# A fused attention and state-space kernel: the third state tile's arguments in full-width matmuls, and a new task order

## The chip, the cores and the metric

The kernel runs on one core of one Trainium2 chip. The metric is the time of one execution on the device in microseconds. A core has TensorE (PE, with weight loads shown apart as PEld), VectorE (DVE), ScalarE (ACT), GpSimd (POOL) and SyncE (SP); the last two mainly issue DMAs here.

## The reference

Two branches work on the same x of 2048 rows and 640 channels, and a gate per row mixes them.

```python
def reference(A_x, A_wqkv, A_wo, ..., B_A_re, B_A_im, B_B_re, ..., B_Dskip, gate_w):
    g = _sigmoid((x * gate_w).sum(-1, keepdims=True))
    a = _A_ref(x, A_wqkv, A_wo)     # local attention: 32 heads of 20, 8 positions with stride 2
    b = _B_ref(x, ...)              # state-space convolution
    return g * a + (1 - g) * b

def _B_ref(u, A_re, A_im, B_re, B_im, C_re, C_im, log_dt, Dskip):
    dt = jnp.exp(log_dt)[:, None]
    logdA = dt * A                  # A, B, C complex, 640 channels x 192 states
    P = jnp.exp(logdA[:, :, None] * l[None, None, :])
    K = jnp.einsum("dn,dnl,dn->dl", Cc, P, dB).real
    # y = causal convolution of u with K along 2048 positions, by FFT
    return y + u * Dskip
```

The edit lies in how K is computed: for every channel, a sum over 192 complex states of exponentials at all positions.

## The kernel before

**Stages.** The state's parameters are prepared by elementwise work and written to a DRAM table `Sprm` (12 numbers per state, 192 states per channel). Then a planned stretch, up to about 302 us, mixes four kinds of work on all engines: the projections to q, k and v (L328), the local attention (products L377 and L442, sums L383 and L447, output projection L464), the kernel K of the state branch (class `KGen`, L768 to L826), and the first step of the FFTs (L1195). After it `fft_conv` does the rest of the convolution and the output in the order of the code.

**The order.** In the planned stretch each piece of work is a `Task` with an engine (or a choice of ACT and DVE for evictions from PSUM), a price in us, what it depends on, the buffers it takes and releases, and a due time. `Plan.order` is a list scheduler run while the program is built: it takes the free engine with the earliest start and, among tasks ready there, the one with the least due time. For tasks with a choice of engine `bd` is added to the due time on DVE and `ba` taken off on ACT; `grace` is added for a ScalarE task that needs another activation table. The dictionary `PLAN` holds these numbers, the due times of the stages and offsets of single tasks (`off`). Each engine then executes its tasks in that fixed order, waiting where an input is not there.

**The K stage.** It runs over 10 chunks. A chunk has 8 channels from each of 8 groups (4 groups `g`, each in two halves `v`), 192 states each. `load_L` fetches the chunk's slice of `Sprm` into a tile L with the DMA queue of SP: partitions 0 to 63 hold groups 0 and 2, partitions 64 to 127 groups 1 and 3. There are two L tiles, so the load of chunk c waits for the arguments of chunk c-2.

192 states are one and a half times 128, so the states of a pair of halves are three tiles `u` of 128 partitions. In the tiles 0 and 1 the first 128 states of one half v fill the partitions. Tile 2 has the remaining 64 states of both halves, 64 partitions each. For each tile and chunk there are four sine tasks and two exponent tasks on PE, named arg: a matmul with 64 rows of L as the stationary operand and a constant matrix R (304 or 216 columns) streaming gives the arguments in PSUM, and ScalarE applies Sin (L785) or Exp (L787) to them in one instruction. Tile 0 and 1 use L768, tile 2 uses L773. DVE multiplies the results (L808 to L810) into `pt` and `qq`, and 64 or 128 small matmuls per tile (L826, in four tasks kmm) sum over the states into `kps`, 32 columns of the array per group g. These small matmuls go in tile order 0, 1, 2 and accumulate in the same PSUM bank; for tiles 0 and 1 they contract 128 rows, for tile 2 64 rows.

The attention weights are stored by SP (aS, L419) and read back spread over partitions (asb, L423), on the same queue as L; results of the attention leave by it too (L484). GpSimd's queue carries q, k, v (L343, L368) and the constants of the FFT.

Of the kernel before, what the change touches and what calls it, by code (L numbers as in the profile page):

```python
# [20 lines left out]
S = 2048  # L21
D = 640
# [14 lines left out]
def _attn_consts():  # L37
# [5 lines left out]
    for wp in range(W):  # L43
# [1 line left out]
    return ind.astype(NPBF), ident.astype(NPBF), mask0  # L45


PLAN = dict(free=dict(P=4.0, A=4.2, D=4.7, S=16.0, G=16.0), phase=0.0, look=0.2, ba=85.1, bd=-687.6, grace=2235.8, p0=-791.4, p1=9.6, tx=[1364.4, 1460.7],
            txw=191.1, ql=135.4, vl=-242.7, pw=18.0, el=-653.5, tl=53.4, vw=216.1, gate=2445.0,
            l=[281.2, 189.1, 532.1, 186.3, 592.1, 47.7, -314.8, 735.8, 829.8, 993.2, 720.0, 710.4], a=[363.0, -174.6, -128.2, 185.6, 703.1, 918.9, 1303.1, 1413.4],  # L50
            v=[-164.3, -448.6, 45.4, 323.3, 710.0, 789.4, 646.8, 1095.8], g=[10.7, 292.0, -348.6, -469.5, -539.5, 427.8, 247.2, -1193.3, -158.0, -278.7, -66.5],
            dl=[129.5, 80.5, 337.8, 725.2, 614.9, 306.3, 515.6, 330.1, 400.6, 420.8],
            kl=[-352.8, -363.0, -133.2, -213.8, -584.9, -123.6, 147.3, -7.2, -17.6, -95.2], Ll=1248.1, argl=366.8, xl=1038.4, c0=1194.1, x0=1143.6, x1=118.9,
            f0=-483.5, f1=51.4, u0=914.8, u1=33.6, off={59: 46.6, 61: 84.7, 94: -58.1, 96: -12.9, 100: -8.6, 102: -29.5, 107: 10.3, 111: 11.8, 113: 8.0, 116: -14.8,
            120: 4.2, 124: -16.2, 129: -52.6, 138: -3.1, 140: -39.7, 146: -5.9, 149: -47.1, 157: -75.2, 160: -33.8, 166: -52.0, 173: 27.0, 175: 23.3, 180: -8.6,
            182: -11.7, 186: 12.8, 188: 5.8, 197: 20.3, 198: -7.7, 201: 130.7, 204: -86.5, 206: -14.4, 208: -15.3, 210: -5.1, 212: 12.5, 215: -21.4, 219: 9.3,
            221: 20.7, 223: -12.2, 433: -31.6, 795: 94.5, 1037: 67.6, 1081: -4.5, 1100: 133.0, 1168: -45.3, 1170: 12.6, 1174: 37.0})


class Task:  # L60
# [434 lines left out]
NST = 192  # L495
# [7 lines left out]
NPC = 12  # L503
# [205 lines left out]
class KGen:  # L709
# [24 lines left out]
    def load_L(self, c):  # L734
        nc = self.nc
        L = self.Lb[c % 2]
        for g in range(4):
            for v in range(2):
                d0 = 160 * g + 80 * v + 8 * c
                src = self.prm.S[d0:d0 + 8].rearrange("(s q) i n -> (q i) s n", q=4)  # L740
                nc.sync.dma_start(L[64 * (g % 2) + 2:64 * (g % 2) + 2 + 4 * NPC, g // 2, :, NST * v:NST * v + NST], src)

    def plan(self, pl, pa, pk, start, hold, params, opened, fin):
        nc, R = self.nc, self.R
# [4 lines left out]
        for c in range(NCH):  # L749
            d0, dd = start(c), start(c + 1) - start(c)  # L750
            L = self.Lb[c % 2]
            Lt = pl.add(f"L{c}", "S", 3.5, lambda _, c=c: self.load_L(c), deps=argt[c - 2] if c > 1 else params, due=d0 - pr["Ll"], dma=1.3)
            argt.append([])
            ends, held, k = {}, {}, 0
            b = {"started": set()}
            for kind in (0, 1) if c % 2 == 0 else (1, 0):
                for u in range(3):
                    ends[u, kind] = []
                    for gp in range(2):
                        for sub in range(2) if kind == 0 else (None,):  # L760
                            def args(_, u=u, kind=kind, gp=gp, sub=sub, b=b, L=L):
                                ar = b["ar"] = pa.tile([128, 2, 512], F32, name="ar")
                                for sb, a0 in ((sub, 0),) if kind == 0 else ((0, 0), (1, EW)):
                                    c0, ncol = ((0, SW), (SW, EW))[kind]
                                    for g2 in range(2):
                                        rows = slice(64 * g2, 64 * g2 + 64)
                                        if u < 2:
                                            nc.tensor.matmul(ar[:, g2, a0:a0 + ncol], L[rows, gp, sb, NST * u:NST * u + 128], R[rows, c0:c0 + ncol],  # L768
                                                             start=True, stop=True, tile_position=(64 * g2, 0))
                                        else:  # L770
                                            m0 = NST * gp + 128
                                            for h in range(2):
                                                nc.tensor.matmul(ar[64 * h:64 * h + 64, g2, a0:a0 + ncol], L[rows, h, sb, m0:m0 + 64], R[rows, c0:c0 + ncol],  # L773
                                                                 start=True, stop=True, tile_position=(64 * g2, 64 * h))
                                b["ar", u, kind, gp, sub] = ar

                            def act(_, u=u, kind=kind, gp=gp, sub=sub, b=b):
                                opened()
                                ar = b.pop(("ar", u, kind, gp, sub))
                                if gp == 0 and not sub:  # L780
                                    b["T", u, kind] = self.ring[kind][self.turn[kind] % len(self.ring[kind])]
                                    self.turn[kind] += 1
                                dst = b["T", u, kind]
                                if kind == 0:
                                    nc.scalar.activation(dst[:, 2 * gp:2 * gp + 2, sub, :], ar[:].bitcast(I16)[:, :, 0:2 * SW:2], ACT.Sin, scale=SCL)  # L785
                                else:
                                    nc.scalar.activation(dst[:, 2 * gp:2 * gp + 2].rearrange("p g s n -> p g (s n)"), ar[:, :, 0:2 * EW], ACT.Exp)  # L787
                            due = d0 + dd * k / 18.0
                            first = not ends[u, kind]
                            a = pl.add(f"arg{c}{kind}{u}{gp}{sub}", "P", ((0.15, 0.15, 0.30), (0.22, 0.22, 0.40))[kind][u], args, deps=[Lt], after=[prevarg] + ([self.moved] if c == HC + 2 else []), acq=["ar"],  # L790
                                       due=due - pr["argl"], eq=(304, 432)[kind])
                            t = pl.add(f"act{c}{kind}{u}{gp}{sub}", "A", (0.62, 0.83)[kind], act, deps=[a], after=[prevact] + (hold if first and kind == 0 and ns == NTR - 1 else []), acq=[("trg", "exq")[kind]] if first else [],
                                       rel=[("ar", a)], due=due, table=("sin", "exp")[kind])
                            if first:
                                held[u, kind] = t
                                ns += kind == 0
                            prevarg, prevact = a, t
                            argt[c].append(a)
                            ends[u, kind].append(t)
                            k += kind + 1  # L800
            for u in range(3):
# [12 lines left out]
                def kmm(_, u=u, b=b, j=0):  # L814
                    if u == 0 and j == 0:
                        b["kps"] = pk.tile([128, 2, 256], F32, name="kps", tag="kb")
                    pt, qq = b["pq", u]
                    kps, started = b["kps"], b["started"]
                    for ql in (2 * j, 2 * j + 1):
                        for v in range(2):  # L820
                            for c2 in ((u,) if u < 2 else (0, 1)):
                                for g in range(4):
                                    r0 = 0 if u < 2 else 64 * (g // 2)
                                    rows = slice(0, 128) if u < 2 else slice(r0, r0 + 64)
                                    k = 8 * (g if u < 2 else 2 * c2 + g % 2) + ql
                                    nc.tensor.matmul(kps[32 * g:32 * g + 32, c2, NM * ql:NM * ql + NM],  # L826
                                                     pt[rows, k, v, :], qq[rows, k, v, :],
                                                     start=(g not in started), stop=(u == 2 and v == 1), skip_group_check=True,
                                                     tile_position=(r0, 32 * g))
                                    started.add(g)  # L830
                due = d0 + dd * (0.55 + 0.16 * u) + pr["dl"][c]
                p = pl.add(f"pq{c}{u}", "D", 2.04, products, deps=ends[u, 0] + ends[u, 1], after=self.pqs[-1:], acq=["pq"], rel=[("trg", held[u, 0]), ("exq", held[u, 1])], due=due)
                self.pqs.append(p)
                for j in range(4):
                    m = pl.add(f"kmm{c}{u}{j}", "P", 0.18 if u < 2 else 0.35, lambda e, kmm=kmm, j=j: kmm(e, j=j), deps=[p], after=[prevkmm], acq=["kb"] if u == 0 and j == 0 else [],
                               rel=[("pq", p)] if j == 3 else [], due=due + pr["kl"][c] + 0.2 * j, eq=211)
                    if u == 0 and j == 0:
                        m0 = m
# [435 lines left out]
```

## Time and profile before

| what | value |
|---|---|
| median of 3 runs | 385.3 us (383.39 to 386.51) |
| the profiled execution | 384.76 us |
| its span, first to last instruction | 383.0 us |
| mean granted TensorE clock | 0.95 |
| PE busy | 316.9 us |
| DVE busy | 323.0 us |
| ACT busy | 304.1 us |

The span is what the profile covers; the execution's own time is 1.76 us longer. Lines such as L768 are lines of the kernel file. Busy time of a group of instructions is the time in which at least one of them ran. A matmul's own duration in the profile (some 300 ns) is much longer than the distance between two starts, since they overlap; the distance in the timeline is what one costs. The word issue as a releaser stands for time in which the engine waited for nothing that the profile shows.

### The profile page before, as it was taken

What the parts mean: (1) busy time and instruction counts of PE and PEld (TensorE: products, weight loads), DVE (VectorE), ACT (ScalarE), POOL (GpSimd) and SP (SyncE); (2) the same over time, 40 slices, a digit from 0 to 9 for tenths busy, and PEclk for the clock granted to TensorE, in tenths of its full rate; (3) what the DMA queues carried; (4) which work ended last, traced back from release to release, by engine and by line L of the source; (5) the groups of instructions that cost most, each with busy time, mean ns of one, the idle gap of its engine ahead of it and who ended that gap; (6) DMA issues with size and microseconds to landing.
All of it is one profiled execution on the core that took longest, in us unless ns stands there. A gap on an engine that the chain in (4) does not pass through costs nothing.

```text
span 383.0 us, 11863 instructions
## 1 busy us (share of the span) xinstructions
PE 316.9 (83%) x5102; PEld 191.0 (50%) x5126; DVE 323.0 (84%) x437; ACT 304.1 (79%) x427; POOL 89.3 (23%) x122
## 2 busy tenths in 40 slices
PE   0268999998999979988997699889999899987760
PEld 0144564433445545444454344557777655656760
DVE  4879997669999989889998799999896389999782
ACT  1699884677979889789879698988987798995890
POOL 8930331140211001513653100100010022000053
PEclk9998999999999999999989757999999999998996
DMA  8982878472645233686455850403740199926056
GB/s 266 373 252 94 246 212 256 117 215 86 193 125 157 64 112 95 158 224 188 104 124 134 274 154 2 151 2 101 254 140 34 36 211 244 207 40 222 2 119 159
DMA packets 51529, 58.84 MB, mean 154 GB/s; under 512 B 36244, under 2 KB 43284, under 8 KB 51220
## 3 DMA queue, kind: packets, MB, share of 16 engines
q1 hardware_dynamic: 41492, 28.78, 28.3%
q0 software_dynamic: 8256, 28.69, 25.6%
q8 instruction: 40, 0.66, 0.7%
q10 hardware_dynamic: 1728, 0.61, 0.7%
q14 instruction: 13, 0.11, 0.1%
HBM read 38.29 MB, written 19.77 MB: 152 GB/s over the span
## 4 chain that ended last, share of the span: by engine, by line
PE 51%; ACT 19%; DVE 13%; DMA 9%; issue 5%; SPq 1%; POOL 1%; POOLq 0%; ACTq 0%; DVEq 0%
PE tb L328 13%; PE tb L447 7%; PE ar L768 6%; PE fp L1024 5%; PE tb L464 5%; PE kps L826 4%; PE bp L1195 3%; DMA aim<-in_B_A_im_dram 3%; ACT big L787 3%; ACT sp_u L1027 3%; ACT big L785 3%; PE lg L383 3%; DVE bufA L985 3%; ACT sp_k L1027 3%; PE ar L773 2%
## 5 line engine op out<-in xcount | busy, mean ns | idle before, releaser
L328 PE MATMUL tb<-bufA 128*128 128x512 bf16 x283 | 71.5, 388 | 6.5 <-DVE bufA L492 2.1
L785 ACT ACTIVATE big<-ar 128x608 bf16<-128x608 int16 x96 | 59.6, 677 | 10.2 <-PE ar L768 9.4
L787 ACT ACTIVATE big<-ar 128x864 bf16<-128x864 f32 x60 | 50.2, 897 | 4.1 <-PE ar L768 3.3
L442 DVE TENSOR_TENSOR pv<-vc,asb 128x2048 bf16<-128x2048 bf16 x40 | 47.2, 1219 | 4.3 <-PE tb L447 2.1
L328 PEld LDWEIGHTS <-bufA 128*128 128x128 bf16 x300 | 33.2, 120 | 35.1 <-issue 12.2
L377 DVE TENSOR_TENSOR prod<-qc,kc 128x2048 bf16<-128x2048 bf16 x40 | 47.9, 1219 | 2.7 <-PE lg L383 2.5
L768 PE MATMUL ar<-Rarg,L 64*128 64x304 bf16 (+1 forms) x320 | 37.0, 290 | 5.8 <-ACT big L785 2.4
L447 PE MATMUL tb<-pv,ident 128*128 128x512 bf16 (+1 forms) x185 | 39.1, 348 | 2.5 <-DVE prj L492 1.0
L826 PE MATMUL kps<-qq,pt 128*32 128x22 bf16 (+1 forms) x2560 | 30.2, 175 | 4.6 <-issue 4.2
L1024 PEld LDWEIGHTS <-PHI 128*128 128x128 bf16 x256 | 24.8, 97 | 17.6 <-issue 7.4
L826 PEld LDWEIGHTS <-pt 128*32 128x32 bf16 (+1 forms) x2560 | 23.3, 93 | 17.5 <-issue 12.3
L464 PE MATMUL tb<-wo_sb,oT 128*128 128x320 bf16 x160 | 27.7, 310 | 0.0
L768 PEld LDWEIGHTS <-L 64*128 64x128 bf16 x320 | 13.7, 94 | 27.7 <-issue 25.3
L447 PEld LDWEIGHTS <-ident 128*128 128x128 bf16 x192 | 17.8, 99 | 17.3 <-issue 5.5
L490 ACT ACTIVATE prj<-tb 128x512 bf16<-128x512 f32 x28 | 16.5, 598 | 10.9 <-PE tb L328 9.9
L959 POOL DMA_DIRECT2D PHI<-c_phi x8 | 4.5, 558 | 79.5 <-PE fp L1024 41.7
L773 PE MATMUL ar<-Rarg,L 64*64 64x304 bf16 (+1 forms) x320 | 19.6, 298 | 3.8 <-ACT big L787 1.6
L1027 ACT ACTIVATE sp_k<-fp 128x1280 bf16<-128x1280 f32 x16 | 19.1, 1236 | 3.3 <-PE fp L1024 3.0
L810 DVE TENSOR_TENSOR qq<-big 128x1408 bf16<-128x1408 bf16 x24 | 21.3, 886 | 0.0
L1024 PE MATMUL fp<-bufA,PHI 128*128 128x320 bf16 x128 | 19.1, 298 | 2.3 <-ACT sp_u L1027 1.5
L243 PE MATMUL ar<-ident,xn 128*128 128x128 bf16 x80 | 7.9, 263 | 15.6 <-DMA xn<-in_A_x_dram 14.1
L1024 PE MATMUL fp<-big,PHI 128*128 128x320 bf16 x128 | 19.2, 298 | 1.8 <-ACT sp_k L1027 1.8
(201 smaller groups left out, 633.0 us busy)
## 6 DMA issues: line engine op xcount, KB each, us to landing
asb<-aS SPq DMA_DIRECT2D x8, 512.0 KB, 4.0
PSI<-c_psi SPq DMA_DIRECT2D x8, 512.0 KB, 10.2
PHI<-c_phi POOLq DMA_DIRECT2D x8, 384.0 KB, 6.6
Sprm<-pc SPq DMA_DIRECT2D x12, 240.0 KB, 3.7
L<-Sprm SPq DMA_DIRECT2D x80, 36.0 KB, 2.6
kc<-kS POOLq DMA_DIRECT2D x8, 337.5 KB, 4.7
vc<-vS POOLq DMA_DIRECT2D x8, 337.5 KB, 4.9
xn<-in_A_x_dram SPq DMA_DIRECT2D x4, 640.0 KB, 12.4
```

Source lines behind the costliest of these rows:

```text
L328: nc.tensor.matmul(ppf, self.wq[:, kt, which * D + e:(which + 1) * D:5], self.xT[:, c0 // 1024, kt, c0 % 1024:c0 % 1024 + SC], start=(kt = ...
L377: nc.vector.tensor_tensor(b[e][:], b["qc"][:, e, :].unsqueeze(1).to_broadcast([128, W, C]), win(b["kc"][:, e, :], 0, W, DIL, C), ALU.mult)
L442: nc.vector.tensor_tensor(b["pv", e][:, :, k, :].rearrange("p w (b t) -> p w b t", t=64), for_e, aw, ALU.mult)
L447: nc.tensor.matmul(b["op", e][:, 0:n, :], ident[:], b["pv", e][:, w, 0:n, :], start=(w == 0), stop=(w == W - 1))
L464: nc.tensor.matmul(apf[:, :320], b["oT"][:, e, i * 128:(i + 1) * 128], wo_sb[:, e, hf * 320:(hf + 1) * 320], start=(e == 0), stop=(e == 4))
L768: nc.tensor.matmul(ar[:, g2, a0:a0 + ncol], L[rows, gp, sb, NST * u:NST * u + 128], R[rows, c0:c0 + ncol], start=True, stop=True, tile_pos ...
L773: nc.tensor.matmul(ar[64 * h:64 * h + 64, g2, a0:a0 + ncol], L[rows, h, sb, m0:m0 + 64], R[rows, c0:c0 + ncol], start=True, stop=True, til ...
L785: nc.scalar.activation(dst[:, 2 * gp:2 * gp + 2, sub, :], ar[:].bitcast(I16)[:, :, 0:2 * SW:2], ACT.Sin, scale=SCL)
L787: nc.scalar.activation(dst[:, 2 * gp:2 * gp + 2].rearrange("p g s n -> p g (s n)"), ar[:, :, 0:2 * EW], ACT.Exp)
L826: nc.tensor.matmul(kps[32 * g:32 * g + 32, c2, NM * ql:NM * ql + NM], pt[rows, k, v, :], qq[rows, k, v, :], start=(g not in started), stop ...
L1024: nc.tensor.matmul(fp[:, fl, 0:320].rearrange("p (c x) -> p c x", x=32), PHI[:, fl, kind, :], B[:, :, 2 * f1 + ri].rearrange("p c q g -> p ...
L1027: nc.scalar.activation(t[:], fp[:, :, 0:320].rearrange("p f (x g) -> p x f g", g=4), ACT.Identity)
```

## The change

The table L is stored in another order. The 384 columns of L for one half v now hold, in this order: the first two groups' states 0 to 127, then their states 128 to 191 beside the last two groups' states 128 to 191, then the last two groups' states 0 to 127. The groups 2 and 3 therefore come in two DMAs each instead of one. Every tile is now 128 adjacent columns of L, and each argument task has the same two (sine) or four (exponent) matmuls with 128 stationary columns; the branch with four 64x64 matmuls is gone. The mixed tile moves from place 2 to place 1. The tiles now hold other groups: tile 0 the groups 0 and 1 with both v, tile 2 the groups 2 and 3, so their small matmuls go to two of the four column strips; tile 1 has all four groups with 64 rows each. Prices in the plan follow, and all numbers of `PLAN` and its offsets are others.

```diff
-PLAN = dict(free=dict(P=4.0, A=4.2, D=4.7, S=16.0, G=16.0), phase=0.0, look=0.2, ba=85.1, bd=-687.6, grace=2235.8, p0=-791.4, p1=9.6, tx=[1364.4, 1460.7],
...
+PLAN = dict(free=dict(P=4.0, A=4.2, D=4.7, S=16.0, G=16.0), phase=0.0, look=0.2, ba=194.5, bd=1544.6, grace=243.1, p0=-727.2, p1=21.0, tx=[-447.7, -203.8],
...
@@ load_L
                 src = self.prm.S[d0:d0 + 8].rearrange("(s q) i n -> (q i) s n", q=4)
-                nc.sync.dma_start(L[64 * (g % 2) + 2:64 * (g % 2) + 2 + 4 * NPC, g // 2, :, NST * v:NST * v + NST], src)
+                dst = L[64 * (g % 2) + 2:64 * (g % 2) + 2 + 4 * NPC, :, v]
+                if g < 2:
+                    nc.sync.dma_start(dst[:, :, 0:NST], src)
+                else:
+                    nc.sync.dma_start(dst[:, :, NST:256], src[:, :, 128:NST])
+                    nc.sync.dma_start(dst[:, :, 256:2 * NST], src[:, :, 0:128])
@@ plan
-            Lt = pl.add(f"L{c}", "S", 3.5, lambda _, c=c: self.load_L(c), ..., dma=1.3)
+            Lt = pl.add(f"L{c}", "S", 5.4, lambda _, c=c: self.load_L(c), ..., dma=1.5)
...
-                                        if u < 2:
-                                            nc.tensor.matmul(ar[:, g2, a0:a0 + ncol], L[rows, gp, sb, NST * u:NST * u + 128], R[rows, c0:c0 + ncol],
-                                                             start=True, stop=True, tile_position=(64 * g2, 0))
-                                        else:
-                                            m0 = NST * gp + 128
-                                            for h in range(2):
-                                                nc.tensor.matmul(ar[64 * h:64 * h + 64, g2, a0:a0 + ncol], L[rows, h, sb, m0:m0 + 64], R[rows, c0:c0 + ncol],
-                                                                 start=True, stop=True, tile_position=(64 * g2, 64 * h))
+                                        nc.tensor.matmul(ar[:, g2, a0:a0 + ncol], L[rows, sb, gp, 128 * u:128 * u + 128], R[rows, c0:c0 + ncol],
+                                                         start=True, stop=True, tile_position=(64 * g2, 0))
...
-                            a = pl.add(f"arg{c}{kind}{u}{gp}{sub}", "P", ((0.15, 0.15, 0.30), (0.22, 0.22, 0.40))[kind][u], args, ...
+                            a = pl.add(f"arg{c}{kind}{u}{gp}{sub}", "P", (0.15, 0.22)[kind], args, ...
...
-                            for c2 in ((u,) if u < 2 else (0, 1)):
-                                for g in range(4):
-                                    r0 = 0 if u < 2 else 64 * (g // 2)
-                                    rows = slice(0, 128) if u < 2 else slice(r0, r0 + 64)
-                                    k = 8 * (g if u < 2 else 2 * c2 + g % 2) + ql
+                            for c2 in range(2):
+                                for g in range(4) if u == 1 else (u, u + 1):
+                                    r0 = 64 * (g // 2) if u == 1 else 0
+                                    rows = slice(r0, r0 + 64) if u == 1 else slice(0, 128)
+                                    k = 8 * (2 * c2 + g % 2) + ql
                                     nc.tensor.matmul(kps[32 * g:32 * g + 32, c2, NM * ql:NM * ql + NM],
                                                      pt[rows, k, v, :], qq[rows, k, v, :],
-                                                     start=(g not in started), stop=(u == 2 and v == 1), skip_group_check=True,
+                                                     start=(g not in started), stop=(v == 1 and u == 1 + g // 2), skip_group_check=True,
                                                      tile_position=(r0, 32 * g))
...
-                    m = pl.add(f"kmm{c}{u}{j}", "P", 0.18 if u < 2 else 0.35, ...
+                    m = pl.add(f"kmm{c}{u}{j}", "P", 0.35 if u == 1 else 0.18, ...
```

## The prediction

> **What bounds the kernel now.** I read the page's head first, then busy time by stretch, then TensorE's groups with shapes kept apart, then the timeline where its clock is full and where it is halved, and last the DMA queue of SyncE. The head, and the groups of the whole span:
>
> ```profile
> span 383.0 us, 11863 instructions
> PE 316.9 (83%) x5102; PEld 191.0 (50%) x5126; DVE 323.0 (84%) x437; ACT 304.1 (79%) x427; POOL 89.3 (23%) x122
> PE 51%; ACT 19%; DVE 13%; DMA 9%; issue 5%; SPq 1%; POOL 1%; POOLq 0%; ACTq 0%; DVEq 0%
> ```
>
> Three engines are near the same load, and the chain that ended last runs half its time through PE. The planned part holds the change; in the busy times by stretch it splits at 258.3 us, where ScalarE ends its last state activation (columns: stretch, length, busy of PE, PEld, DVE, ACT, POOL, clock, DMA share, GB/s):
>
> ```profile
> 75.00:258.30 183.30, 164.10 (x3607) 85.34 (x3620) 166.63 (x234) 156.74 (x232) 40.28 (x48) 0.93 0.48 134
> 258.30:302.00 43.70, 41.84 (x435) 31.99 (x437) 36.70 (x48) 36.14 (x46) 2.66 (x4) 1.00 0.37 116
> ```
>
> No engine alone sets the first stretch: DVE 91%, PE 90%, ACT 86% of it. The second is PE's, 96% of it. From 302 us on the code is the same. So a saving on PE is worth its full length only where it lets work come forward out of the second stretch.
>
> **The argument matmuls** (L768 tiles 0 and 1, L773 tile 2), in TensorE's groups by shape:
>
> ```profile
> L768 PE MATMUL ar<-Rarg,L 64*128 64x304 bf16 x160 | 23.8, 319 | 4.2 <-ACT big L785 2.4 <-ACT bufA L785 1.2
> L773 PE MATMUL ar<-Rarg,L 64*64 64x304 bf16 x160 | 12.5, 334 | 1.6 <-ACT big L785 1.1
> L768 PE MATMUL ar<-Rarg,L 64*128 64x216 bf16 x160 | 13.2, 261 | 1.6 <-ACT big L787 1.0 <-DVE nxt L492 0.4
> L773 PE MATMUL ar<-Rarg,L 64*64 64x216 bf16 x160 | 7.1, 262 | 2.3 <-ACT big L787 1.6 <-issue 0.5
> L826 PE MATMUL kps<-qq,pt 128*32 128x22 bf16 x1280 | 15.6, 177 | 0.2 <-DVE qq L810 0.2
> L259 PE MATMUL ar<-gw_sb,bufA 128*128 128x1 bf16 x80 | 2.1, 163 | 0.0
> ```
>
> A sine task of tile 0 or 1 is 2 matmuls, so 80 tasks took 23.8 us, 0.298 each; one of tile 2 is 4 matmuls, 40 tasks took 12.5 us, 0.313 each. Exponent tasks: 40 in 13.2 us (0.330) against 20 in 7.1 us (0.355). The four quarter-size matmuls already run beside each other; the third tile is not twice as dear, though the plan has it at 0.30 and 0.40 against 0.15 and 0.22. Making tile tasks alike saves 40 x 0.015 + 20 x 0.025 = 1.1 us of PE in the whole kernel. If every task gained as much as one whole short matmul start of the nearest row (L259, 2.1 us / 80 = 26 ns), the 160 removed matmuls would be worth 4.2 us; that is the far bound. On the other side the saving is nothing, where ACT is what PE waits for (4.2 + 1.6 + 1.6 + 2.3 us of idle stand before these groups, mostly ACT's). I take -0.8, near the direct rows. The 160 weight loads that go with them overlap matmuls and cost nothing; the cover is PEld at 85.3 of 183.3 us, and without it they would be a gain (8.9 us for 320, so 4.5 us).
>
> The Trainium skill ("TensorE: Matmul & The Clock Gate", Wait — 56ns, not 53.3ns?) says starts never come closer than about 25 ns, however short the matmul. By that the sum of this step would be -4.0 instead of -0.8; the trace agrees on the whole array (26 ns above) and disagrees for tiles, as the next lines show.
>
> **The matmuls that form K** (L826). Before, tiles 0 and 1 send each step to all four 32-column strips; after, tiles 0 and 2 use strips 0, 1 or 2, 3, each twice in turn, and tile 1 has the four strips with 64 rows. The counts are the same: 16, 32 and 16 per piece. Timeline, at full clock (190 us) and at half clock (216 us):
>
> ```profile
> 190.02 0.37 PE L826 MATMUL kps<-qq,pt 64*32 64x22 bf16 x32
> 190.36 0.31 PE L768 MATMUL ar<-Rarg,L 64*128 64x304 bf16 x2
> 190.59 0.61 PE L383 MATMUL lg<-prod,ind 128*32 128x512 bf16 x8
> ...
> 191.37 0.37 PE L826 MATMUL kps<-qq,pt 128*32 128x22 bf16 x32
> 191.68 0.30 PE L768 MATMUL ar<-Rarg,L 64*128 64x304 bf16 x2
> 215.88 0.41 PE L826 MATMUL kps<-qq,pt 64*32 64x22 bf16 x33 [2.61 <-issue]
> ...
> 216.59 0.40 PE L826 MATMUL kps<-qq,pt 64*32 64x22 bf16 x32
> 216.92 0.43 PE L768 MATMUL ar<-Rarg,L 64*128 64x304 bf16 x2
> ```
>
> Start to next start: 0.34 us / 32 = 10.6 ns and 0.31 / 32 = 9.7 at full clock, 0.33 / 32 = 10.3 at half clock. A pace that does not move when the clock halves is not set by streaming 22 columns, so four strips are more than it needs, and I cost two strips at nothing. Lower bound: nothing, as no work goes. Upper bound: each matmul waits for its predecessor as on the whole array, 26 ns: 10 chunks x 2 tiles x 64 = 1280 matmuls, each 15.7 ns longer, 20 us of PE. Between these the rows nearest in kind are the 10 ns ones.
>
> **The loads of the table L** (L741). Before 8 DMAs per chunk; after, the upper two groups are cut in two, 12 per chunk. All 40 new ones are issued on SP's queue, POOL's is untouched. From the source view of that line (its instruction, who waited for it in us and times, and landing):
>
> ```profile
> L741 SPq DMA_DIRECT2D L<-Sprm x80: 302/423/1613, 62.6 to 226.7; - x80
> PEld L768: 0.6, 2
> DMA to landing us min/median/max: 1.7/2.6/5.1
> ```
>
> At the median of 423 ns, 4 more are 1.7 us per chunk and 17 us of SP in all. PE waited for a load of L twice, 0.6 us. L for chunk 7 is issued from 184.8 to 189.6 us and first used at 205.1, so 1.7 us hides behind 15 us of the chunk before. What stands behind it on SP is the pair of transfers that spread the attention weights (aS, then asb); at 207.65 an aS store follows an L burst at once. If all 8 blocks stood behind one and DVE had nothing else, 8 x 1.7 = 13.6 us; nothing where they don't. DVE's wait for asb is 1.8 us today, so I take 0. The pieces shrink from rows of 384 bytes to 256 and 128 for half the groups, 36 KB per DMA becoming 24 and 12, hidden by the same lead.
>
> **The order anew.** No task is added or removed; their fixed order is recomputed from new prices and priorities. Evictions that either engine may do lose rank on DVE (bd from -687.6 to 1544.6) and gain it on ACT (ba 85.1 to 194.5), a change of activation table costs less rank (grace 2235.8 to 243.1). DVE was busy 203.3 and ACT 192.9 of the 227 us from 75 to 302, so evening them out is worth up to 5.2 us. 10 ACT table loads stand at the state's two activation lines, at 1.283 us; twice as many would cost ACT 12.8 us, against 34 us idle. PE idles 21.1 us in those 227. The profile cannot say which order is better; its bounds are the cases below, and I take 0.
>
> **Sum.** -0.8 (arguments) + 0 (K) + 0 (loads) + 0 (order) on the profiled execution's own 384.76 us (span 383.0 and 1.76 around it) gives 384.0. The median of the three runs, 385.3, is 0.5 above that execution. Runs differ by 383.39 to 386.51, so about 1% is what a measurement tells from no change.
>
> **Rivals.** *The order fits better*: the 2.61 us in which PE and then every engine waited for issue at 213 us, and the halved clock after it, are not met again, and DVE sheds evictions: 384.0 - 2.6 - 5.2 = 376.2, say 377. For it: 24 us of DVE idle in 227; the clock was halved from 215 to 232 us, where sine tasks took 0.43 us instead of 0.30. Against: DVE was full through that stretch, so the half clock cost little, and the stall ends in issue, which an order does not address.
>
> *The order is built on PE time that does not exist* (slower): the plan's price of the arguments falls by 40 x 0.15 + 20 x 0.18 = 9.6 us, PE's work by 1.1. The other 8.5 us is filled with tasks that come late. In-order queues pass that on: behind a late argument matmul stand ACT's next activation, then DVE's products. Place: the arguments from 75 to 258 us, where ACT already waits 9.4 us for L768. It decides once PE's idle time at those places (9.7 us before the four argument groups) is used up. All of it on the path: 384.0 + 8.5 = 392.5. Against: 21 us of PE idle could take it.
>
> *Two strips are too few* for L826: the 20 us above, of which PE's half of the chain would show, 384.0 + 10 = 394. Against it: the pace at half clock. If 26 ns held for one strip only, two in turn would give 13 ns, 1280 x 2.7 ns = 3.5 us, 386 to 387. By the same section of the skill's page a floor kept by each strip gives this last figure.
>
> *It does not do what it says*: the third tile's tasks are already as short as the others; this is in the forecast, not a separate case.
>
> **How the numbers follow.** Forecast, no measurable change: 0.34, own range 381 to 388. Better order 0.31. Late arguments 0.22. Strips 0.13. The better order may go beyond 377 and the two slower ones may add; I leave 1 in 10 out on each side: 375 to 396. Faster by over 1%: 0.31 + 0.01 of the forecast = 0.32. Slower by over 1%: 0.21 + 0.12 + 0.02 = 0.35. Within: 0.33.
>
> **What would show it.** L768 should have 480 matmuls: 240 of 304 columns near 35.7 us busy and 240 of 216 columns near 19.8; L773's line gone. L826 stays near 10 ns from start to start; 13 or more says strips. 120 issues at L741, with PE's wait for L under 2 us. If ACT's wait for argument matmuls grows well past its 15.9 us (9.4 + 3.3 + 2.3 for L768, 0.7 + 0.2 for L773), the late-argument rival is right. If DVE's idle in the planned part shrinks by 5 us or ACT does more of the evictions, the better order. The forecast is wrong if the planned part, now ending at 302 us, moves by over 4 us.

## The result, and the profile after

The changed kernel takes 401.6 us (median of 4 runs, 400.35 to 405.11) against 385.1 us for the kernel before (4 runs, 383.39 to 386.51). The ratio is 1.0445, 95% interval 1.0363 to 1.0527: slower, where the forecast was 384.0 and the range ended at 396. The profiled execution took 400.35 us, its span is 398.3, 15.3 longer than before. Medians count every run; the ratios leave out runs over 1.5% above the fastest of their kernel.

The head of the page after, with its row of the granted clock in 40 slices (here some 10 us each) and the shares of the chain that ended last:

```profile
span 398.3 us, 11631 instructions
PE 335.4 (84%) x4966; PEld 199.2 (50%) x4966; DVE 319.7 (80%) x428; ACT 316.3 (79%) x438; POOL 83.0 (21%) x122
...
PEclk9999999999999998688955558989999999996996
...
PE 61%; ACT 23%; issue 5%; DMA 4%; DVE 3%; POOL 1%; SPq 1%; POOLq 0%; ACTq 0%
```

The clock row before, for comparison:

```profile
PEclk9998999999999999999989757999999999998996
```

The records hold 136 PE matmuls fewer, and PE is busy 18.5 us longer. Its share of the chain went from 51% to 61%. The clock row after shows a run of fives around 200 to 240 us that the kernel before does not have (its mean clock was 0.950, this one's is 0.906).

The planned part now ends at about 316.8 us instead of 302.0 (its last L1195 matmul at 315.7 instead of 300.6), so nearly all of the 15.3 us lie in it. Its busy times by stretch (stretch, length, busy of PE, PEld, DVE, ACT, POOL, clock, DMA share, GB/s), and the second stretch in the kernel before:

```profile
75.00:316.80 241.80, 219.91 (x3882) 122.25 (x3881) 199.67 (x272) 201.00 (x285) 34.54 (x49) 0.87 0.43 119
200.00:241.00 41.00, 34.12 (x936) 18.35 (x928) 32.89 (x54) 34.27 (x49) 2.35 (x4) 0.50 0.39 110
```

```profile
200.00:241.00 41.00, 33.83 (x815) 16.77 (x814) 35.98 (x52) 34.07 (x50) 6.63 (x12) 0.73 0.49 140
```

PE's idle time in the planned part is 241.8 - 219.9 = 21.9 us; before it was 227.0 - 205.9 = 21.1. So PE does not wait more: it is busy 14.0 us longer with fewer matmuls. Where, say its groups by shape, and the K group of 64 rows in the kernel before:

```profile
L773 PE MATMUL ar<-Rarg,L 64*128 64x304 bf16 x240 | 39.7, 342 | 6.1 <-ACT big L785 3.6 <-ACT bufA L785 1.1 <-ACT big L787 0.9
L826 PE MATMUL kps<-qq,pt 128*32 128x22 bf16 x1280 | 24.9, 176 | 5.5 <-issue 5.5
L773 PE MATMUL ar<-Rarg,L 64*128 64x216 bf16 x240 | 22.9, 284 | 3.3 <-ACT big L787 3.2
L826 PE MATMUL kps<-qq,pt 64*32 64x22 bf16 x1280 | 14.7, 174 | 4.6 <-issue 4.6
```

```profile
L826 PE MATMUL kps<-qq,pt 64*32 64x22 bf16 x1280 | 14.6, 173 | 4.3 <-issue 4.2
```

Two things stand out. The K matmuls of 128 rows took 15.6 us before and take 24.9; those of 64 rows, which still rotate over four strips, took 14.6 and now 14.7. And the argument matmuls take 62.6 us where 35.7 + 19.8 were expected. The timeline of PE, first where the clock is full and then at 223 us, shows both the slower pace and a third thing:

```profile
119.97 0.56 PE L826 MATMUL kps<-qq,pt 128*32 128x22 bf16 x32
120.47 0.30 PE L773 MATMUL ar<-Rarg,L 64*128 64x304 bf16 x2
...
223.54 0.31 PE L826 MATMUL kps<-qq,pt 128*32 128x22 bf16 x10
226.06 0.26 PE L826 MATMUL kps<-qq,pt 128*32 128x22 bf16 x6 [2.21 <-issue]
```

32 K matmuls of 128 rows on two strips last 0.56 us from the first start to the last end; in the kernel before 32 of them on four strips took 0.37 (at 191 us). And in the middle of a run of K matmuls PE stops for 2.21 us on nothing that the profile shows.

**What the stalls are.** In every kernel here, all PE stalls of over 0.45 us before an instruction that waits for no semaphore stand at one and the same remainder when PE's recorded instructions are counted in steps of 256 (a few records are missing, so the remainder drifts by up to 8 within a run). The trace's DMA records have a queue that the page calls q8 instruction; it moves packets of 16,384 bytes, and 39 of them over the run fit PE's 4966 + 4966 instructions in blocks of 256 (38.8). So I read these stalls as ends of a block of the instruction stream: the next block isn't there yet. In all runs here two of these packets never start closer together than 3.28 us. A block of K matmuls alone is 128 matmuls with their weight loads, which take 128 x 7 to 13 ns = 0.9 to 1.7 us, so PE can run ahead of its instructions. The Trainium skill ("Runtime: NRT & Kernel Launch", Instruction fetch mechanics) has the same block, 16 KiB or 256 instructions, and calls the cost of crossing its end "mostly hidden"; the trace agrees on the size and not on the cost, 10.1 us of stalls here.

**What the half clock is.** The trace's clock records say 0.5 or 1.0. From 75 to 317 us the spells at 0.5 last multiples of 3.4 us and sum to 23.9 us before and 61.4 after, 41.0 of it in one spell from 200.3 us. Of the 20 spells of 10 us or more in that stretch of all runs here, 15 begin 1 to 4 us after the start of a stall of over 0.45 us (in the changed kernel a stall from 196.6 to 198.5, then the spell from 200.3); the other five don't. The Trainium skill ("TensorE: Matmul & The Clock Gate", Part 1: The HAM clock gate) describes this gate, half or full by how busy PE was in the last 3.4 us; the lengths of the spells agree. What counts as busy is the question of experiment 9.

Three suspects, then: the strips, the block ends, the order that meets the half clock. The table sums up the runs that follow. Stalls are those of at least 0.15 us without a wait; stalls and half clock are summed from 75 to 317 us of each profiled run. The forms of the runs are explained below; o_old and o_new stand for the old and the new order.

| kernel | median us | ratio to before (95%) | K of 128 rows, busy | stalls | half clock |
|---|---|---|---|---|---|
| before | 385.1 | | 15.6 | 6.2 | 23.9 |
| after | 401.6 | 1.0445 (1.0363 to 1.0527) | 24.9 | 10.1 | 61.4 |
| s_new_o_old | 392.8 | 1.0209 (1.0121 to 1.0298) | 23.5 | 9.2 | 37.5 |
| s_old_o_new | 394.6 | 1.0253 (1.0189 to 1.0317) | 17.1 | 10.2 | 58.0 |
| s_fix_o_old | 386.3 | 1.0015 (0.9968 to 1.0062) | 15.9 | 3.7 | 17.1 |
| s_fix_o_new | 399.5 | 1.0374 (1.0283 to 1.0466) | 17.4 | 15.6 | 54.6 |
| s_fix_8_loads | 388.55 | 1.0030 (0.9992 to 1.0068) | 15.9 | 7.2 | 23.9 |
| s_one_strip | 404.5 | 1.0480 (1.0422 to 1.0537) | 30.4 | 9.0 | 44.4 |
| before, moved by 112 | 401.5 | 1.0395 (1.0349 to 1.0441) | 15.9 | 12.3 | 44.4 |
| before, moved by 160 | 390.0 | 1.0109 (1.0017 to 1.0202) | 16.0 | 8.7 | 27.3 |
| before, moved by 224 | 388.9 | none on record | 15.8 | 7.1 | 20.5 |
| after, moved by 16 | 403.0 | 1.0447 (1.0354 to 1.0540) | 24.9 | 9.9 | 61.4 |
| after, moved by 144 | 404.9 | 1.0495 (1.0400 to 1.0591) | 24.4 | 11.4 | 61.4 |

### The profile page after: what moved, and what is told of

Its sections match the earlier page's. It is cut to its first block, busy times and chain, and to the rows that moved or that the text cites. A ratio compares the mean times of both kernels' runs of the same rounds, so it can differ in the third digit from the quotient of the medians.

```text
span 398.3 us, 11631 instructions
## 1 busy us (share of the span) xinstructions
PE 335.4 (84%) x4966; PEld 199.2 (50%) x4966; DVE 319.7 (80%) x428; ACT 316.3 (79%) x438; POOL 83.0 (21%) x122
## 4 chain that ended last, share of the span: by engine, by line
PE 61%; ACT 23%; issue 5%; DMA 4%; DVE 3%; POOL 1%; SPq 1%; POOLq 0%; ACTq 0%
PE tb L329 12%; PE ar L773 10%; PE tb L448 9%; PE kps L826 8%; PE tb L465 5%; PE fp L1024 5%; PE bp L1195 4%; DMA aim<-in_B_A_im_dram 3%; PE lg L384 3%; ACT big L785 3%; ACT sp_u L1027 3%; ACT big L787 3%; ACT sp_k L1027 3%; ACT big L491 2%; PE cp L1057 2%
## 5 line engine op out<-in xcount | busy, mean ns | idle before, releaser
L329 PE MATMUL tb<-bufA 128*128 128x512 bf16 x300 | 72.4, 386 | 1.1 <-DVE bufA L493 0.5
L785 ACT ACTIVATE big<-ar 128x608 bf16<-128x608 int16 x96 | 61.1, 678 | 13.6 <-PE ar L773 12.0
L773 PE MATMUL ar<-Rarg,L 64*128 64x304 bf16 (+1 forms) x480 | 62.2, 313 | 9.4 <-ACT big L787 4.1
L826 PE MATMUL kps<-qq,pt 128*32 128x22 bf16 (+1 forms) x2560 | 39.3, 175 | 10.1 <-issue 10.1
L826 PEld LDWEIGHTS <-pt 128*32 128x32 bf16 (+1 forms) x2560 | 31.3, 95 | 25.7 <-issue 21.6
L448 PE MATMUL tb<-pv,ident 128*128 128x512 bf16 (+1 forms) x192 | 42.3, 368 | 0.0
L773 PEld LDWEIGHTS <-L 64*128 64x128 bf16 x480 | 20.7, 97 | 42.7 <-issue 38.6
L465 PE MATMUL tb<-wo_sb,oT 128*128 128x320 bf16 x160 | 28.7, 317 | 0.1
L491 ACT ACTIVATE prj<-tb 128x512 bf16<-128x512 f32 x33 | 19.4, 597 | 11.1 <-PE tb L329 9.6
L448 PEld LDWEIGHTS <-ident 128*128 128x128 bf16 x192 | 18.5, 103 | 17.3 <-issue 5.9
L808 DVE TENSOR_TENSOR pt<-big 128x1024 bf16<-128x1024 bf16 x24 | 16.5, 689 | 6.6 <-PE kps L826 4.4
## 6 DMA issues: line engine op xcount, KB each, us to landing
PHI<-c_phi POOLq DMA_DIRECT2D x8, 384.0 KB, 5.6
```

What stands on the lines that cost most here:

```text
L329: nc.tensor.matmul(ppf, self.wq[:, kt, which * D + e:(which + 1) * D:5], self.xT[:, c0 // 1024, kt, c0 % 1024:c0 % 1024 + SC], start=(kt = ...
L448: nc.tensor.matmul(b["op", e][:, 0:n, :], ident[:], b["pv", e][:, w, 0:n, :], start=(w == 0), stop=(w == W - 1))
L465: nc.tensor.matmul(apf[:, :320], b["oT"][:, e, i * 128:(i + 1) * 128], wo_sb[:, e, hf * 320:(hf + 1) * 320], start=(e == 0), stop=(e == 4))
L491: nc.scalar.activation(o, i, ACT.Identity)
L773: nc.tensor.matmul(ar[:, g2, a0:a0 + ncol], L[rows, sb, gp, 128 * u:128 * u + 128], R[rows, c0:c0 + ncol], start=True, stop=True, tile_pos ...
```

## The experiments

**1. The content in the old order.** The whole change, but with the numbers of `PLAN` and the task prices of the kernel before. The cut compares it with the changed kernel.

```diff
-PLAN = dict(..., ba=194.5, bd=1544.6, grace=243.1, p0=-727.2, p1=21.0, ...
+PLAN = dict(..., ba=85.1, bd=-687.6, grace=2235.8, p0=-791.4, p1=9.6, ...
-  "P", (0.15, 0.22)[kind], args, ...
+  "P", ((0.15, 0.15, 0.30), (0.22, 0.22, 0.40))[kind][u], args, ...
```

> The whole change except the order: the new table, full-width argument matmuls and two strips per small-matmul tile, with the plan's numbers and prices of before, so that the tasks stand in the order of before. Strip theory (the 128-row matmuls of L826 start every 12.8 ns in the trace of after against 7.0 before, 1280 of them: 7.4 us of TensorE, and the halved clock follows from it): slower, 393 to 401 us. Order theory (the loss is the new order's): within 1% of before, 384 to 388 us. Half and half: near 392 us.

It took 392.8 us (391.29 to 396.66), 1.0209. Its groups by shape:

```profile
L772 PE MATMUL ar<-Rarg,L 64*128 64x304 bf16 x240 | 35.6, 327 | 3.7 <-ACT big L784 1.7 <-ACT bufA L784 1.2
L825 PE MATMUL kps<-qq,pt 128*32 128x22 bf16 x1280 | 23.5, 175 | 0.0
L772 PE MATMUL ar<-Rarg,L 64*128 64x216 bf16 x240 | 19.8, 263 | 3.2 <-ACT big L786 2.1 <-DVE nxt L492 0.4 <-issue 0.4
```

In this order the arguments cost 35.6 + 19.8 us, as the prediction had it (35.7 and 19.8); the K matmuls keep their extra 8 us. So with the content alone, in the old order, the kernel loses 2.1% where the whole change loses 4.5%.

**2. The new order with the old content.** The kernel before with `PLAN` and prices of after. The mixed tile, still with four 64x64 matmuls, stands at place 1, since the new order counts on it there.

```diff
-  if u < 2:
-      nc.tensor.matmul(ar[...], L[rows, gp, sb, NST * u:NST * u + 128], ...
+  if u != 1:
+      nc.tensor.matmul(ar[...], L[rows, gp, sb, NST * (u // 2):NST * (u // 2) + 128], ...
...
-  for c2 in ((u,) if u < 2 else (0, 1)):
+  for c2 in ((u // 2,) if u != 1 else (0, 1)):
```

> The new order alone: plan numbers and prices of after, the mixed tile at place 1 as that order expects, but the table, the loads, the four 64x64 matmuls and the four strips of before. Strip theory: about the time of before, 384 to 388 us. Order theory: near the time of after, 397 to 402 us. Half and half: near 392 us.

394.6 us (393.95 to 396.66), 1.0253, with K at 17.1 us and 58.0 us of half clock. The order alone, on work that is otherwise as before, loses 2.5%: 8.2 us against the median of before among these runs (386.4). That lies between the two expectations.

**3. and 4. Full-width arguments and the new table with four strips.** The edit's first aim without the strips: the groups of the tiles stay as before, so that each K step still goes to all four column strips, and the arguments are 128 columns wide from the new table with 12 loads. Once in each order. The cuts compare it with the changed kernel.

```diff
-  nc.tensor.matmul(ar[...], L[rows, sb, gp, 128 * u:128 * u + 128], R[...], ...
+  lh = L[rows, sb, u, 256 * gp:256 * gp + 128] if u < 2 else L[rows, sb, gp, 128:256]
+  nc.tensor.matmul(ar[...], lh, R[...], ...
...
-  for c2 in range(2):
-      for g in range(4) if u == 1 else (u, u + 1):
+  for c2 in ((u,) if u < 2 else (0, 1)):
+      for g in range(4):
```

(In the new order `u != 1` and `u // 2` take the place of `u < 2` and `u`.)

> The new table with its 12 loads and the full-width argument matmuls, in the order of before, but the tiles chosen so that tiles 0 and 1 again hold all four groups of one half: same table, other columns of it, small matmuls as before on four strips. If the stated purpose (argument matmuls) is worth what its rows say, 384 us, 1 us less than before. If the 40 added loads cost anything, 387 us or more, with TensorE waiting for L over 2 us. Strip and order theory both expect no loss here.

> As the run before this one (new table, full-width argument matmuls, four strips), but in the order of after, with the mixed tile at place 1. Strip theory: 383 to 386 us. Order theory: 396 to 401 us. Half and half: near 392 us. Against after itself it prices the strips under the new order: 7 us or more less if they are a cost of their own.

In the old order: 386.3 us (10 runs), 1.0015, no measurable change. So the full-width arguments, the new table and its loads show neither a cost nor a gain there. Against experiment 1, which differs in the tiles' groups and the mixed tile's place, the gap is 392.8 - 386.3 = 6.5 us, near the gap in K's busy time (23.5 - 15.9 = 7.6). But the stalls (9.2 against 3.7 us) and the half clock (37.5 against 17.1) differ too, and experiment 7 shows that the place of the block ends alone can cost more than 6.5 us. So the slower K matmuls are shown, and that they make up the 6.5 us is not. In the new order: 399.5 us, though its K matmuls are as fast as before's. The waits of PE in this run:

```profile
PE kps L827 <- issue: 15.6, 8, 3.7
```

Eight stalls, 15.6 us, where the changed kernel has 10.1. In the new order the two medians lie only 401.6 - 399.5 = 2.1 us apart, and the intervals of the two ratios overlap. A possible reason, which no run tests: with two strips a block of K matmuls lasts longer, so PE outruns its instructions less. The two gaps do not add up either: strips alone and order alone would make 6.5 + 13.2 = 19.7 us on top of experiment 3; the changed kernel has 401.6 - 386.3 = 15.3. Experiments 1 to 4 ran each content in each order at one place of the block ends only.

**5. Fewer loads.** `s_fix_o_old` with 8 loads per chunk in place of 12: the upper groups are brought in one DMA each, into the same bytes of the tile.

```diff
-  if g < 2:
-      nc.sync.dma_start(dst[:, :, 0:NST], src)
-  else:
-      nc.sync.dma_start(dst[:, :, NST:256], src[:, :, 128:NST])
-      nc.sync.dma_start(dst[:, :, 256:2 * NST], src[:, :, 0:128])
+  nc.sync.dma_start(dst[:, :, NST * (g // 2):NST * (g // 2) + NST], src)
```

The upper groups' half tile then holds states 0 to 63 and their full tile 64 to 191. Each state is still taken once, so the sum and the amount of work are the same.

> Full-width argument matmuls, four strips and the order of before again, but the table is loaded with 8 DMAs per chunk: the states of groups 2 and 3 are laid in the same columns without turning them, so that their half tile is states 0 to 63 and their full tile 64 to 191 (a sum over states does not mind). Against the run with 12 loads in the same order it prices the 40 added DMAs: if they cost what DVE waited more for transfers there (two waits of 3 to 4 us before the attention products), 380 to 384 us and the best version; if they are hidden, the same time, 385 to 387 us.

388.55 us (12 runs) beside 386.27 for 12 loads: not faster with fewer. The 40 added DMAs show no cost, though stalls and half clock differ here too (table).

**6. One strip at a time.** The kernel of experiment 1, with the 128-row K matmuls sorted by strip: eight in a row on one, then eight on the other.

```diff
+  todo = [(g, ql, v, c2) for ql in (2 * j, 2 * j + 1) for v in range(2) for c2 in range(2) for g in (range(4) if u == 1 else (u, u + 1))]
+  if u != 1:
+      todo.sort(key=lambda t: t[0])
```

> The whole change in the order of before, but the small matmuls of the tiles 0 and 2 go through one strip after the other (8 in a row on one strip) instead of two in turn. Floor-per-strip theory: each of the 1280 starts about 25 ns after the one before (12.8 ns with two strips, 7.0 with four), so their busy time grows from 23.5 to about 37 us and the time to 400 us or more. If the pace with two strips comes from something else (the issue, PSUM), it stays near 12.8 ns and 393 us.

404.5 us, 1.048. The group by shape:

```profile
L825 PE MATMUL kps<-qq,pt 128*32 128x22 bf16 x1280 | 30.4, 176 | 0.0
```

The mean distance between starts is 7.1 ns on four strips in turn (before), 12.9 on two, 18.5 here, while the 64-row ones, which this edit leaves alone, stay at 7.4. The trace does not name the strips, but their order is known: on two strips the distances are 3 and 22 ns in turn, on four 3, 4, 3 and 15, so a strip comes round again after 25 to 28 ns (9 of 10 turns on two strips, 6 of 10 on four) and almost never sooner. I read this as a floor for each strip, which rotation hides; no run tells a strip of the array from the 32 PSUM partitions that it writes. I had expected 37 us busy for a full 25 ns; the direction was right, the size too large. In this run over a third of the distances are 24 to 28 ns, and most others are about 20 and about 5 in turn, which make 25 together, as if the two strips overlapped where the code sorts them; that stays unexplained. Beside experiment 1, with nearly the same stalls (9.0 against 9.2), K is busy 6.9 us longer and the kernel takes 404.5 - 392.8 = 11.7 us longer. Of all pairs here this one shows best that slower strips cost time.

**7. Block ends alone.** The kernel before with tiny matmuls added near its start, into a PSUM place that holds nothing needed any more. Each is a weight load and a matmul, so 56 of them move every later block end by 112 instructions, 80 by 160, 112 by 224. They lie in 9.5 us in which PE waits for x anyway.

```diff
+  for _ in range(56):      # 80, 112 in the other two
+      nc.tensor.matmul(lt[:, 1, 0:10], lg10[:], ident[0:10, 0:10], start=True, stop=True)
```

> The kernel before with 56 tiny matmuls (10 columns, 112 instructions with their weight loads) added to TensorE's stream while it waits for the first rows of x, 2.6 to 15 us, where they cost nothing. Nothing else is touched; every later TensorE instruction stands 112 places further in the stream. Fetch theory (TensorE's stalls without a wait lie at the ends of blocks of 256 instructions, where the next block has not come yet, and hurt where a block is mostly small matmuls): the stalls move to other instructions, their recorded place again at one remainder of 256; by the distances in the trace of before they grow from 3.9 to about 9 us, and with more half clock after them the time is 390 to 397 us. If the stalls belong to the places in the program (to DMA traffic or to what is computed there) or are of no account: within 1% of before.

> The same with 80 tiny matmuls (160 instructions), between the two others in number. The count gives 9.1 us of stalls against 4.2. Fetch theory: 394 to 402 us. If the place of the block ends does not matter or the added number decides: between the two others in order of their number.

> The kernel before with 112 tiny matmuls (224 instructions) in TensorE's first idle stretch, so that all block ends move. From the trace of before, counting for every block how much less than 3.4 us (the shortest fetch seen) its 256 instructions take, the stalls sum to 3.2 us at this shift against 4.2 unshifted and 10.5 at the shift of 112 that took 16 us more. Fetch theory: within 1% of before, 382 to 388 us, not slower, though twice as many instructions are added as in the slow one. If the added instructions themselves cost: 400 us or more.

With 112 instructions: 401.5 us (400.69 to 407.27), 1.0395 (1.0349 to 1.0441), some 15 us lost by nothing but this. Its waits of PE, and the timeline of one of its stalls:

```profile
PE kps L828 <- issue: 10.8, 8, 2.2
```

```profile
224.51 0.21 PE L828 MATMUL kps<-qq,pt 64*32 64x22 bf16 x7
226.94 0.88 PE L828 MATMUL kps<-qq,pt 64*32 64x22 bf16 x89 [2.21 <-issue]
```

Stalls rose from 6.2 to 12.3 us and the half clock from 23.9 to 44.4. With 224 instructions, twice the added work, it took 388.9 us (four runs, 383.67 to 394.65; the kernel before beside it 383.62 to 390.75), so it is the place of the block ends that costs, not the added matmuls. The number of 16,384-byte packets follows too: 41 in that run, for 10,476 instructions recorded (40.9 blocks). With 160 I had expected 394 to 402 from a count of blocks that K matmuls fill; it took 390.0, 1.0109. With 224 the count gave 3.2 us of stalls and 7.1 were measured. So the count picked the worst of these places, and gave neither the stalls nor the time.

**8. Is the new order's loss such an accident?** The same shift in the changed kernel, by 16 and by 144 instructions.

> The kernel after with 8 tiny matmuls (16 instructions) in TensorE's first idle stretch. The count of short blocks gives 4.0 us against 4.8 unshifted. If the new order's loss is mostly the chance of where its block ends fall: 396 to 401 us. If nothing in it hangs on that: 401 us.

> The kernel after with 72 tiny matmuls (144 instructions). The count gives 7.7 us against 4.8, the worst place of that order. Fetch theory: 403 to 412 us. If the new order is slow whatever the place of the block ends: 401 us.

403.0 us (1.0447) and 404.9 us (1.0495); the first was expected at 396 to 401 if the loss were mostly such a chance. The half clock was 61.4 us in all three alignments. So the new order's long half-clock spells do not hang on one unlucky block end. But in none of the five kernels with the new order and no idle matmuls are the stalls under 9.9 us, so no run shows that order without them.

**9. Can the half clock be driven out?** The changed kernel with 224 idle matmuls of 160 columns added after K pieces of four chunks, into columns of PSUM that nobody reads. Once on the whole array, once on 128 rows and 32 columns of it.

```diff
+  if 4 <= c < 8 and len(started) == 4:
+      for _ in range(7):
+          nc.tensor.matmul(kps[0:128, :, 176:256], R[:, 0:128], R[:, 0:160]..., start=False, stop=False, ...)
```

> The kernel after with 7 idle matmuls of 160 columns on the whole 128x128 array behind each of the last 8 small-matmul pieces of chunks 4 to 7 (results go to unused columns of the PSUM bank). They add 224 x 67 ns = 15 us of TensorE at full clock, 30 at half. If the halved clock stays because the work of that stretch (arguments on 64 rows, small matmuls on 32 columns) fills little of the array, the 41 us at half clock from 200 to 241 shrink to under 20 us and the time is 400 to 410 us although work was added. If the clock follows only how long TensorE runs, which it did 8 to 9 tenths of that stretch, the half clock stays near 60 us in all and the time is 418 to 430 us.

> The same 224 idle matmuls with the same 160 columns, the same number of instructions at the same places, but on 128x32 of the array. If the share of the array counts: the half clock stays near 60 us or grows, the added work runs at half pace, 415 to 430 us, clearly above the run with the whole array. If only running time or the place of the instructions counts: the same as that run within 1%.

414.3 us (1.0673) and 409.3 us (1.0542). From 200 to 241 us, on the whole array and then on one strip:

```profile
200.00:241.00 41.00, 33.83 (x894) 23.96 (x894) 27.84 (x47) 28.00 (x40) 2.35 (x4) 0.96 0.41 111
```

```profile
200.00:241.00 41.00, 31.79 (x852) 21.91 (x850) 26.73 (x45) 27.59 (x40) 2.36 (x4) 0.85 0.37 107
```

The clock there rose from 0.50 to 0.96 and 0.85, and the half clock from 75 to 317 us fell from 61.4 to 30.7 and 34.1 us. Both releases cost more than they brought; 414.3 lies between the two ranges that were expected of the first run. The idle matmuls also move the block ends behind them, but three other alignments of this kernel kept 61.4 us of half clock. I had held that the gate goes by the share of the array in use, which the strip run should not have changed; that fell. The profile's busy share does not tell it either: the stretch at half clock has PE busy for 34.12 of 41 us, the one at 0.96 for 33.83, and the same stretch of the kernel before, at 0.73, also for 33.83. From the first run a price can be estimated: its idle matmuls were busy 22.5 us, and the span grew by 12.6, so up to 10 us came back for 30.7 us less of half clock, a third of a microsecond for each. From the first idle matmul to the next piece of work they held PE for 20.3 us only, and 2.1 us of the gain are fewer stalls (10.1 to 8.0); that way it is a fifth.

## Why the prediction was wrong, step by step

**K matmuls, costed at 0.** This is the step of the sum that failed: "A pace that does not move when the clock halves is not set by streaming 22 columns, so four strips are more than it needs". The first half held; the second does not follow. What fits the paces on four, on two and on sorted strips is a floor of each strip, some 25 ns, which four strips in turn hide. The 10 ns base was too high as well, since it divided by the count across the edges of other tasks; start to start within a run it was 7.1. So the term is 1280 x (13 - 7) = 7.7 us of PE instead of 0. The gap in time in the old order is 6.5 us (experiments 1 and 3), with the stalls and the half clock grown as well. The rival's smaller version had the mechanism (26 ns for one strip, 13 for two) and priced it at 3.5 us from that base. The Trainium skill's floor of about 25 ns between starts ("TensorE: Matmul & The Clock Gate", Wait — 56ns, not 53.3ns?) is not kept by the kernel as a whole here, where starts on different strips come 3 ns apart; 25 to 28 ns is what the trace shows for each strip, which that section does not say.

**The order, costed at 0 with bounds from two rivals.** This failed too, as a term put at nothing though the profile "cannot say which order is better": the runs with the new order took 8.2 us more with the old content and 13.2 us more (399.5 against 386.3) with full-width arguments on four strips. Each is one place of the block ends, and such a place alone moved the old order by up to 15 us (experiment 7). The signs do not fit "late arguments". That rival decides once PE's idle time before the argument matmuls is used up, and of 9.7 us 9.4 are left (6.1 + 3.3). PE did not wait more in all (21.9 us idle against 21.1). The sign that was to prove it, ACT's waits for argument matmuls, did grow, 15.9 to 23.7 us; but it was 25.9 in the kernel before with shifted block ends, whose order is the old one, so it does not tell that rival from any other slower PE. No run gave the old order the new prices alone, so what the prices did to the order stays open. The better order's premise, DVE and ACT evened out, came true (203.3 to 199.7 and 192.9 to 201.0) and no gain shows.

What goes with the new order in every run is the clock: from 200 to 241 us it is 0.50 to 0.59 in the five kernels with the new order and no idle matmuls, and 0.70 to 0.88 in the eight with the old one. "DVE was full through that stretch, so the half clock cost little" was where I could have seen the risk: I took the half clock as a given of 17 us (20.5 in the records) that costs little, and not as something that a new order can lengthen. At a fifth to a third of a microsecond for each, 61.4 - 23.9 = 37.5 us more would be worth some 7 to 12 us, an estimate that overlaps with the stalls.

**Issue stalls.** The prediction let the 2.61 us at 213 us vanish in one rival and called them something "which an order does not address". An edit that moves instructions on PE's queue moves the block ends, and 112 instructions did it for some 15 us; in the changed kernel the stalls grew from 6.2 to 10.1 us.

**Arguments, -0.8.** Right by the rows: 35.6 + 19.8 = 55.4 us busy in the old order (experiment 1) after 56.6 before. In the changed kernel they took 39.7 + 22.9, and many of them lie in the half clock, where their mean rises from 342 and 284 ns to 429 and 367 (200 to 241 us). And the saving did not reach the end of the kernel, 1.0015 in experiment 3.

**Loads, 0.** Right: 120 issues on SP at about the same median (380 to 428 ns by line against 423), PE waits 1.2 us in all for L, and eight loads per chunk were not faster. They landed later (3.8 to 4.6 us by line against 2.6), which the lead hid.

**Open.** Why the kernels with the new order stay at half clock between 200 and 241 us is read from the groups only: in that stretch PE has 60 + 48 argument matmuls of 64 rows and 792 K matmuls, with 8 of L448 and 16 of L384, where the kernel before has 15 of L447, 28 of L383 and 16 of L464. That fits a stretch with too little to stream, and the idle matmuls released it, but no run moved the attention's matmuls back. Of the 16.9 us by which the span of experiment 7's first run is longer, some 6 are stalls and 4 to 7 the half clock by the price above; the rest isn't accounted for. How the loss of the whole change divides among strips, stalls and half clock is not shown. No version was faster than the kernel before.

## What to carry to other kernels

Short matmuls on column strips should rotate over all the strips there are: the pace per strip had a floor here, and a layout that makes one kind of matmul wider can take strips from another. Runs of tiny matmuls outran their own instruction stream here, so an edit that only moves or removes instructions can cost several per cent; spreading them among longer ones suggests itself but was not tried here. Compare a change, and each part of it, at two or three alignments before judging it. Read the granted clock by stretch before calling half clock free: most long spells here began within 4 us of the start of a stall, and the kernels of one order stayed in them for up to 41 us.

## What the runs showed of the hardware that was not expected

- A column strip of TensorE took a new matmul of 22 columns every 25 to 28 ns at best; four strips in turn give 7.1 ns from start to start, two 13, eight in a row on one 18.5.
- PE's instructions seem to come in blocks of 16,384 bytes (39 packets for 38.8 blocks of 256), and two such packets started at least 3.28 us apart; at a block end inside a run of tiny matmuls PE stood up to 4.3 us with nothing to wait for (the run with 8 loads). The kernel before, with 112 harmless instructions added, took some 15 us longer.
- The half clock lasted 41 us in a stretch in which the profile calls PE 83% busy, and idle matmuls of 160 columns, on the whole array or on a quarter of it, ended most of it.
